# Two pairs of heads behind one exponential: four PSUM banks in one tile

## The chip, the cores and the metric

The program runs on one core of one Trainium2 chip. The metric is the device time of one execution in microseconds; the kernel before takes 1420.18 us (median of 3 runs, 1420.05 to 1421.76). A profile of one further execution is read beside it. Engines are named as in the profile: PE is the matrix engine (PEld its weight loads), ACT the engine that evaluates the exponentials, DVE the vector engine, POOL the engine that does the causal masks here, SP the queue that issues most of the DMAs.

## The reference

Two attentions over 2048 tokens with 32 heads of 18 dimensions are computed and their outputs laid side by side. A has one shared key and value head; B is causal inside four segments of 512 tokens and adds a linear memory of the segments before.

```python
# A
scores = jnp.einsum("bhqd,bkd->bhqk", q, k) * (Dh ** -0.5)
p = _softmax(scores, axis=-1)
o = jnp.einsum("bhqk,bkd->bhqd", p, v)
# B, for each segment s
logits = jnp.einsum("bhqd,bhkd->bhqk", qs, ks) * scale + mask
p = _softmax(logits, axis=-1)
a_dot = jnp.einsum("bhqk,bhkd->bhqd", p, vs)
o = g * a_mem + (1.0 - g) * a_dot
```

## The kernel before

The first 290 us or so are the projections of A and B. What the change touches is the attention stage behind them, one straight line of instructions whose order on PE, ACT and DVE is written out by hand (`tc.manual_schedule`), engine by engine. A planner places semaphores and hands out buffers: an instruction that writes a tile for the first time waits until one of the tile's buffers has been read by its last reader.

**Blocks.** There are 32 A blocks (4 chunks of 512 queries, 8 groups of 4 heads) and 32 B blocks (4 segments, 8 groups), set one behind the other in the list `blocks`. In a block the work is cut into *items*: one key tile `kt` of 128 keys and one *pair* of heads, `pr` 0 or 1. An A block has 16 x 2 = 32 items, in the order (kt 0, pr 0), (kt 0, pr 1), (kt 1, pr 0) and so on, a B block 3 x 2 = 6.

**Turns.** Items are taken three at a time (`turns`, made by `split`, lines 1080 to 1096). An A block has ten turns of three and, last, one of two: turns 0 to 10 in this text. A B block has two turns of three, 0 and 1. There are 416 turns. In turn k the loop at line 1111 issues, in this order: the scores of the turn's items (PE), the exponentials (ACT), one step of an output projection of finished work (tile F; its eight matmuls are line 770), one step of an exponential that DVE computes by a polynomial (`slow`), and the products of turn k-2 (PE, line 967).

**Scores.** `scores()` writes the two heads of a pair into a PSUM tile `E` of two banks, 128 keys by 2 x 512 queries: two matmuls side by side in the array, each preceded by its weight load (line 919 for A, 928 for B). The pool `psE` holds three such tiles; tiles O (products) and F take the other two of the eight banks. The exponential (line 937) reads `E` and writes an SBUF tile `P`, of which there are `PBUFS` = 9. Of a turn's three items the middle one (`i == 1`, `copied`) is first copied by DVE into an SBUF tile `W` (line 934), which frees its banks, and its exponential reads `W`. ACT takes a turn's exponentials in the order 0, 2, 1 (line 1114). Item (kt 0, pr 1) of each A block, the middle one of turn 0, has no ACT exponential; DVE computes it in nine operations spread over the following turns into tile `PD`.

**Products.** `products(b, m, hf)` takes step m of a block and one half `hf` of the queries: four matmul calls, two heads of pair 0 and two of pair 1 (eight matmul instructions in the trace, here called a *group*), so a turn's products are three groups, 24 instructions. In A the key tile of step m is `turn_of[j // 2][m]`: for pair 0 it is m; for pair 1 the list starts at 1 (1, 2, ..., 12, 0, 13, 14, 15), since the DVE item comes late. Steps are cut into threes as the items are, except that the short one lies at place 8 (`prods`, cut two turns earlier). The last group that reads a `P` tile is what gives that buffer back.

**The end.** After the last turn the last two rows of A are projected with the tiles `E`, O and F as accumulators (line 1164), and the results leave through `P`, `W` and `osb`.

Of the kernel before, what the change touches and what calls it, by code (L numbers as in the profile page):

```python
# [7 lines left out]
F32 = mybir.dt.float32  # L8
F32R = mybir.dt.float32r
# [21 lines left out]
PBUFS = 9  # L31
# [40 lines left out]
def attention_pair_kernel(ctx, tc, a_xT, a_w, a_wo, b_xT, b_w, b_wo, b_beta, ident_d, hmask_d, bmask_d, cmask_d, sel_d, zmask_d, selx_d, sely_d, out):  # L72
# [601 lines left out]
    psE = ctx.enter_context(tc.tile_pool(name="psE", bufs=3, space=PSUM))  # L674
# [231 lines left out]
    def scores(it, pr, copied):  # L906

        ab, c, hg, kt = it
        st = stacks[ab, c, hg // 2]
        h = 2 * (hg % 2) + pr  # L910
        e = psE.tile([128, 2, 512], F32, name="E")
        dve = ab == "A" and (kt, pr) in BY_DVE
        p = pp.tile([128, 2, 512], F32, name="PD" if dve else "P", bufs=1 if dve else PBUFS)
        state[it, pr] = p
        n = 512 if ab == "A" else 512 - 128 * kt if kt < 2 else 384
        if ab == "A":
            for j, r0 in enumerate(HALF):
                rows = slice(r0, r0 + KR)
                nc.tensor.matmul(e[:, j], kstA[rows, 128 * kt : 128 * kt + 128], st[rows, h, :], start=True, stop=True)  # L919
            if (kt, pr) in BY_DVE:  # L920
                exponentials(p, e)
                return lambda: None
        else:
            for k, c0 in BKEYS[kt]:
                ks = slice(128 * k, 128 * k + 128)
                for j, r0 in enumerate(HALF):
                    rows = slice(r0, r0 + KR)
                    nc.tensor.matmul(  # L928
                        e[:, j, c0 : c0 + 512 - 128 * k], st[rows, 4 + h, ks], st[rows, h, 128 * k :], start=True, stop=True
                    )  # L930
        src = e
        if copied:
            src = pp.tile([128, 2, 512], F32, name="W", bufs=2)
            nc.vector.tensor_copy(src[:, :, :n], e[:, :, :n])  # L934

        def exponential():
            nc.scalar.activation(p[:, :, :n], src[:, :, :n], AF.Exp, scale=SCALE)  # L937
            if ab == "B":

                m = len(BKEYS[kt])  # L940
                diag = p.rearrange("p a (b t) -> p a b t", t=256)[:, :, 0:m, 0:128]
                nc.gpsimd.affine_select(  # L942
                    diag, diag, pattern=[[0, 2], [0, m], [1, 128]], base=0, channel_multiplier=-1, compare_op=ALU.is_ge, fill=0.0
                )

        return exponential
# [140 lines left out]
    with tc.manual_schedule(engines={ENG.PE, ENG.Activation, ENG.DVE}):  # L1087
# [23 lines left out]
        for k in range(len(turns) + 2):  # L1111
            now[0] = k
            exps = [scores(its[n], pr, i == 1) for i, (n, pr) in enumerate(turns[k])] if k < len(turns) else []
            for i in (0, 2, 1) if len(exps) == 3 else range(len(exps)):
                exps[i]()
# [36 lines left out]

        def halve_heads(key, t):
            R = RT[t]
            x = halves_of[key, t] = pp.tile([128, 2, 512], F32R, name="P", bufs=PBUFS)
            halve(x[:R, 0], x[:R, 1], parts[key][:R, t])
# [27 lines left out]
        for n, key in enumerate(rows):  # L1184
            end = key == rows[-1]
            banks = [psE.tile([128, 2, 512], F32, name="E") for _ in range(3)]
            dst = [bk[:, hf, :288] for bk in banks for hf in range(2)]
# [8 lines left out]
            for i in range(4):  # L1196
                if end:
                    osb = pp.tile([128, 2, 512], F32, name="P", bufs=PBUFS)[:, :, :288]
                elif i < 2:
                    osb = pp.tile([128, 2, 512], F32, name="W", bufs=2)[:, :, :288]  # L1200
                else:
                    osb = pa.tile([128, D], F32, name="osb", bufs=2).rearrange("p (f n) -> p f n", f=2)
# [60 lines left out]
```

## Time and profile before

| | us |
|---|---|
| runs, median (lowest to highest) | 1420.18 (1420.05 to 1421.76) |
| the profiled execution, its own time | 1422.46 |
| span of its instructions | 1420.8 |
| DVE busy | 1034.9 |
| POOL busy | 248.5 |
| first to last score matmul of the attention stage | 292.8 to 1376.1 |

The profile is of one execution. A row of a group gives line, engine, operation, the tiles (written <- read), shapes and count, then the busy time, the mean duration of one in ns, and the engine's idle time just before them with what ended it. A row of the timeline gives start, length, engine, line and tiles, the number of instructions merged (x2), and in brackets the idle time before them. A timeline asked for a very short stretch shows the instructions that cross it, so single instructions can be told apart. Matmuls are pipelined and their ends are modelled, so a busy PE is not PE at its peak.

### The profile page before, as it was taken

The page shows a single profiled execution, that of the slowest core. Times are in us where ns is not written, and L with a number is a line of the kernel's source. Part 1 is how long each engine was busy: PE and PEld are TensorE (multiplying, and loading weights), DVE is VectorE, ACT ScalarE, POOL GpSimd, SP SyncE. Part 2 cuts the span into 40 slices and gives each one's busy share as a digit, 9 for nine tenths or more (in the row PEclk, how much of TensorE's full clock was granted, in tenths as well). Part 3 has the DMA queues.
Part 4 walks back from the last instruction along what each step waited for, and adds up shares of the span by engine and source line. Part 5 has one row for each costly group of instructions (what it writes and reads, how often), then busy time and mean ns, then how long its engine had stood idle before and what let it go on. Part 6 is the DMA issues. An engine that isn't in the chain of part 4 may idle for free.

```text
span 1420.8 us, 40029 instructions
## 1 busy us (share of the span) xinstructions
PE 1404.1 (99%) x17132; PEld 844.8 (59%) x17132; DVE 1034.9 (73%) x1220; ACT 1205.0 (85%) x1448; POOL 248.5 (17%) x326
## 2 busy tenths in 40 slices
PE   9999999999999999999999999999999999999998
PEld 6788888745555555555555555555555555555558
DVE  6656456467787778877777888777778877887773
ACT  4543434479999999999999999999999999999991
POOL 2431000003313214221110160131011400100002
PEclk9999999999999999999999999999999999999999
DMA  9866546467565535332312542232104121110013
GB/s 271 268 207 187 166 144 219 168 175 223 154 212 160 168 117 162 90 113 77 111 58 70 165 131 91 67 107 75 51 34 135 64 75 47 59 44 18 9 60 111
DMA packets 90720, 172.63 MB, mean 122 GB/s; under 512 B 14576, under 2 KB 22889, under 8 KB 90110
## 3 DMA queue, kind: packets, MB, share of 16 engines
q1 hardware_dynamic: 83978, 159.75, 35.9%
q0 software_dynamic: 1664, 4.78, 1.3%
q10 hardware_dynamic: 4896, 5.51, 1.1%
q8 instruction: 135, 2.21, 0.7%
q14 instruction: 47, 0.39, 0.1%
HBM read 99.32 MB, written 70.67 MB: 120 GB/s over the span
## 4 chain that ended last, share of the span: by engine, by line
PE 67%; ACT 9%; issue 2%; DVE 1%; DMA 0%; POOL 0%; ACTq 0%; DVEq 0%
PE O L967 30%; PE E L919 19%; PE F L770 11%; ACT P L937 9%; PE E L928 3%; PE E L1164 2%; PE F L826 1%; DVE W L934 0%; DMA oA<-oe 0%; PE F L1164 0%; PE O L1164 0%; DMA sm<-oA 0%; POOL P L942 0%; DVE osb L794 0%; DVE o L831 0%
## 5 line engine op out<-in xcount | busy, mean ns | idle before, releaser
L937 ACT ACTIVATE P<-E 128x1024 f32<-128x1024 f32 (+1 forms) x800 | 781.7, 1062 | 11.7 <-PE E L919 11.6
L934 DVE COPY W<-E 128x1024 f32<-128x1024 f32 (+1 forms) x384 | 461.0, 1200 | 176.3 <-PE E L919 120.1
L967 PE MATMUL O<-P,VA 128*32 128x256 f32 x7936 | 508.3, 379 | 0.0
L937 ACT ACTIVATE P<-W 128x1024 f32<-128x1024 f32 (+1 forms) x384 | 427.9, 1114 | 3.9 <-DVE W L934 3.7
L967 PEld LDWEIGHTS O<-P,VA 128*32 128x32 f32 x7936 | 262.6, 110 | 146.5 <-issue 5.7
L919 PE MATMUL E<-stA,kstA 56*128 56x512 f32 x1920 | 329.0, 439 | 2.3 <-DVE W L934 1.3
L919 PEld LDWEIGHTS E<-stA,kstA 56*128 56x128 f32 x1920 | 154.9, 184 | 178.1 <-ACT P L937 112.4
L942 POOL TENSOR_SCALAR_AFFINE_SELECT P<-P 128x256 f32<-128x256 f32 (+1 forms) x192 | 94.6, 493 | 474.0 <-ACT P L937 441.5
L758 POOL TENSOR_TENSOR o<-o,rb 126x512 f32<-126x512 f32 (+1 forms) x55 | 81.9, 1504 | 410.2 <-DMA o<-oA 263.8
L770 PE MATMUL F<-woB,o 126*32 126x192 f32 (+1 forms) x1920 | 127.4, 338 | 0.3 <-DVE osb L794 0.3
L899 DVE SCALAR_TENSOR_TENSOR q<-q,PD 128x1024 f32<-128x1024 f32 x96 | 120.3, 1253 | 0.0
L967 PE MATMUL O<-P,vseg 128*32 128x256 f32 (+2 forms) x1536 | 81.8, 344 | 0.4 <-issue 0.3
L770 PEld LDWEIGHTS F<-woB,o 126*32 126x32 f32 (+1 forms) x1920 | 38.2, 108 | 70.7 <-issue 62.7
L976 DVE COPY oe<-O 128x512 f32<-128x512 f32 x64 | 44.2, 691 | 40.7 <-PE O L967 40.0
L249 PE MATMUL pj<-xh,wBl 128*126 128x512 f32 x180 | 72.4, 403 | 0.0
L249 PE MATMUL pj<-xh,wBh 128*126 128x512 f32 x180 | 71.8, 400 | 0.0
L118 ACT CAST qp<-pj 126x512 fp32r<-126x512 f32 (+1 forms) x54 | 30.9, 584 | 44.7 <-DVE kmB L447 32.9
L770 PE MATMUL F<-woA,o 126*32 126x192 f32 (+1 forms) x960 | 63.9, 338 | 0.0
L967 PEld LDWEIGHTS O<-P,vseg 128*32 128x32 f32 x1536 | 49.0, 109 | 24.9 <-issue 2.0
L928 PE MATMUL E<-stB 56*128 56x256 f32 (+3 forms) x512 | 61.2, 347 | 1.3 <-ACT P L937 0.9
L119 DVE TENSOR_TENSOR qp<-pj,qp 126x512 fp32r<-126x512 f32 (+1 forms) x54 | 36.6, 684 | 35.4 <-ACT qp L118 35.2
L249 PE MATMUL pj<-xl,wBh 128*126 128x512 f32 x144 | 57.3, 399 | 0.0
(193 smaller groups left out, 1388.6 us busy)
## 6 DMA issues: line engine op xcount, KB each, us to landing
stB<-kB SPq DMA_DIRECT2D x96, 144.0 KB
stB<-qB SPq DMA_DIRECT2D x32, 288.0 KB
stA<-qA SPq DMA_DIRECT2D x30, 288.0 KB
oA<-oe SPq DMA_DIRECT2D x32, 256.0 KB
oB<-oe SPq DMA_DIRECT2D x32, 256.0 KB
qA<-qp SPq DMA_DIRECT2D x16, 504.0 KB
kB<-qp SPq DMA_DIRECT2D x16, 504.0 KB
qB<-qp SPq DMA_DIRECT2D x16, 504.0 KB
```

The source lines that it names most:

```text
L119: hold(nc.vector.tensor_tensor(qp[:R, 1, :n], src, qp[:R, 0, :n].bitcast(F32), op=ALU.subtract))
L249: nc.tensor.matmul(dst, w[:, c0 : c0 + M], x, start=i == 0, stop=i == len(ops) - 1)
L758: return lambda: tc.keep_in_program_order(nc.gpsimd.tensor_tensor(dst, a, b, op=op))
L770: nc.tensor.matmul(dst[32 * j : 32 * j + 32], parts[ab, c][: RT[t], t, r0 : r0 + 32], wo[ab][: RT[t], t, c0 : c0 + n], start=start, stop=stop,
L899: steps.append(lambda a=a: v.scalar_tensor_tensor(q, q, a, p, op0=ALU.add, op1=ALU.mult))
L919: nc.tensor.matmul(e[:, j], kstA[rows, 128 * kt : 128 * kt + 128], st[rows, h, :], start=True, stop=True)
L928: nc.tensor.matmul(e[:, j, c0 : c0 + 512 - 128 * k], st[rows, 4 + h, ks], st[rows, h, 128 * k :], start=True, stop=True)
L934: nc.vector.tensor_copy(src[:, :, :n], e[:, :, :n])
L937: nc.scalar.activation(p[:, :, :n], src[:, :, :n], AF.Exp, scale=SCALE)
L942: nc.gpsimd.affine_select(diag, diag, pattern=[[0, 2], [0, m], [1, 128]], base=0, channel_multiplier=-1, compare_op=ALU.is_ge, fill=0.0)
L967: nc.tensor.matmul(o[32 * j : 32 * j + 32, q0 : q0 + n], v, p[:, j % 2, p0 : p0 + n], start=m == hf == 0, stop=last and hf == 1,)
L976: nc.vector.tensor_copy(osb, o)
```

## The change

The three two-bank tiles become one tile `E4` of four banks and one tile `E2` of two, each with a single buffer. A turn's scores go, first, for one item into `E2` (the middle one in an A turn of three, the last one in a B turn; none in a turn of two), then for the two others into the halves of `E4`. One exponential of 4 x 512 columns reads `E4` and writes an SBUF tile `P4` of twice the size. The single item keeps its way through `W` by DVE and its own exponential, now into `P2`, or DVE's polynomial. `P4` and `P2` have three buffers each, the space that nine `P` took. A turn of two has no copy any more. B's masks follow the joint exponential. At the end the accumulators are `E4` and `E2` in place of three `E`, and the last outputs leave through `W` and `osb` alone.

```diff
@@ -28,7 +28,7 @@
 BOUND_UP = 1.0 + 2.0 ** -6
 
 BOUND_OK = 30.0 / SCALE / BOUND_UP
-PBUFS = 9
+PBUFS = 3
 KP = 54
 KR = 56
 VW = DH + 1
@@ -671,7 +671,7 @@
 
     pp = ctx.enter_context(tc.tile_pool(name="pp", bufs=1))
     pa = ctx.enter_context(tc.tile_pool(name="pa", bufs=1))
-    psE = ctx.enter_context(tc.tile_pool(name="psE", bufs=3, space=PSUM))
+    psE = ctx.enter_context(tc.tile_pool(name="psE", bufs=1, space=PSUM))
     psO = ctx.enter_context(tc.tile_pool(name="psO", bufs=1, space=PSUM))
 
     def load_stackA(c, q4):
@@ -903,47 +903,76 @@
         ]
         slow.extend((now[0] + 2 + i, p, step) for i, step in enumerate(steps))
 
-    def scores(it, pr, copied):
+    def width(it):
+
+        return 512 if it[0] == "A" else 512 - 128 * it[3] if it[3] < 2 else 384
+
+    def score(it, pr, e):
 
         ab, c, hg, kt = it
         st = stacks[ab, c, hg // 2]
         h = 2 * (hg % 2) + pr
-        e = psE.tile([128, 2, 512], F32, name="E")
-        dve = ab == "A" and (kt, pr) in BY_DVE
-        p = pp.tile([128, 2, 512], F32, name="PD" if dve else "P", bufs=1 if dve else PBUFS)
-        state[it, pr] = p
-        n = 512 if ab == "A" else 512 - 128 * kt if kt < 2 else 384
         if ab == "A":
             for j, r0 in enumerate(HALF):
                 rows = slice(r0, r0 + KR)
                 nc.tensor.matmul(e[:, j], kstA[rows, 128 * kt : 128 * kt + 128], st[rows, h, :], start=True, stop=True)
-            if (kt, pr) in BY_DVE:
-                exponentials(p, e)
-                return lambda: None
-        else:
-            for k, c0 in BKEYS[kt]:
-                ks = slice(128 * k, 128 * k + 128)
-                for j, r0 in enumerate(HALF):
-                    rows = slice(r0, r0 + KR)
-                    nc.tensor.matmul(
-                        e[:, j, c0 : c0 + 512 - 128 * k], st[rows, 4 + h, ks], st[rows, h, 128 * k :], start=True, stop=True
-                    )
-        src = e
-        if copied:
-            src = pp.tile([128, 2, 512], F32, name="W", bufs=2)
-            nc.vector.tensor_copy(src[:, :, :n], e[:, :, :n])
+            return
+        for k, c0 in BKEYS[kt]:
+            ks = slice(128 * k, 128 * k + 128)
+            for j, r0 in enumerate(HALF):
+                rows = slice(r0, r0 + KR)
+                nc.tensor.matmul(
+                    e[:, j, c0 : c0 + 512 - 128 * k], st[rows, 4 + h, ks], st[rows, h, 128 * k :], start=True, stop=True
+                )
+
+    def mask(it, p):
+
+        if it[0] == "B":
+            m = len(BKEYS[it[3]])
+            diag = p.rearrange("p a (b t) -> p a b t", t=256)[:, :, 0:m, 0:128]
+            nc.gpsimd.affine_select(
+                diag, diag, pattern=[[0, 2], [0, m], [1, 128]], base=0, channel_multiplier=-1, compare_op=ALU.is_ge, fill=0.0
+            )
+
+    def scores(items):
+
+
+        two, one = ((0, 2), 1) if items[0][0][0] == "A" and len(items) == 3 else ((0, 1), 2)
+        if one < len(items):
+
+            it1, pr1 = items[one]
+            e1 = psE.tile([128, 2, 512], F32, name="E2")
+            score(it1, pr1, e1)
+        e = psE.tile([128, 4, 512], F32, name="E4")
+        p = pp.tile([128, 4, 512], F32, name="P4", bufs=PBUFS)
+        pair = [(items[i], p[:, 2 * x : 2 * x + 2]) for x, i in enumerate(two)]
+        for x, ((it, pr), px) in enumerate(pair):
+            state[it, pr] = px
+            score(it, pr, e[:, 2 * x : 2 * x + 2])
+        n = width(items[0][0])
+        assert width(items[two[1]][0]) == n
 
         def exponential():
-            nc.scalar.activation(p[:, :, :n], src[:, :, :n], AF.Exp, scale=SCALE)
-            if ab == "B":
-
-                m = len(BKEYS[kt])
-                diag = p.rearrange("p a (b t) -> p a b t", t=256)[:, :, 0:m, 0:128]
-                nc.gpsimd.affine_select(
-                    diag, diag, pattern=[[0, 2], [0, m], [1, 128]], base=0, channel_multiplier=-1, compare_op=ALU.is_ge, fill=0.0
-                )
-
-        return exponential
+            nc.scalar.activation(p[:, :, :n], e[:, :, :n], AF.Exp, scale=SCALE)
+            for (it, pr), px in pair:
+                mask(it, px)
+
+        if one >= len(items):
+            return [exponential]
+        m = width(it1)
+        if it1[0] == "A" and (it1[3], pr1) in BY_DVE:
+            p1 = state[it1, pr1] = pp.tile([128, 2, 512], F32, name="PD", bufs=1)
+            exponentials(p1, e1)
+            return [exponential]
+        p1 = state[it1, pr1] = pp.tile([128, 2, 512], F32, name="P2", bufs=PBUFS)
+        src = pp.tile([128, 2, 512], F32, name="W", bufs=2)
+        nc.vector.tensor_copy(src[:, :, :m], e1[:, :, :m])
+
+        def exponential1():
+            nc.scalar.activation(p1[:, :, :m], src[:, :, :m], AF.Exp, scale=SCALE)
+            mask(it1, p1)
+
+        return [exponential, exponential1]
 
     acc = {}
 
@@ -1110,9 +1139,8 @@
         wparts = []
         for k in range(len(turns) + 2):
             now[0] = k
-            exps = [scores(its[n], pr, i == 1) for i, (n, pr) in enumerate(turns[k])] if k < len(turns) else []
-            for i in (0, 2, 1) if len(exps) == 3 else range(len(exps)):
-                exps[i]()
+            for step in scores([(its[n], pr) for n, pr in turns[k]]) if k < len(turns) else []:
+                step()
             if memory is None:
                 run_fill()
             elif k >= ASK and all(its[n][0] == "A" for n, pr in turns[k]) and next(memory, None) is None:
@@ -1150,9 +1178,18 @@
         assert len(rows) == 2 and all(ab == "A" for ab, c in rows)
         halves_of = {}
 
+        spare = []
+
         def halve_heads(key, t):
             R = RT[t]
-            x = halves_of[key, t] = pp.tile([128, 2, 512], F32R, name="P", bufs=PBUFS)
+            if not spare:
+
+                if len(halves_of) == 6:
+                    spare.extend(pp.tile([128, 2, 512], F32R, name="P2", bufs=PBUFS) for _ in range(3))
+                else:
+                    x = pp.tile([128, 4, 512], F32R, name="P4", bufs=PBUFS)
+                    spare.extend((x[:, 0:2], x[:, 2:4]))
+            x = halves_of[key, t] = spare.pop(0)
             halve(x[:R, 0], x[:R, 1], parts[key][:R, t])
 
         def multiply(key, t, dst):
@@ -1183,8 +1220,8 @@
             halve_heads(rows[1], t)
         for n, key in enumerate(rows):
             end = key == rows[-1]
-            banks = [psE.tile([128, 2, 512], F32, name="E") for _ in range(3)]
-            dst = [bk[:, hf, :288] for bk in banks for hf in range(2)]
+            banks = [psE.tile([128, n, 512], F32, name=f"E{n}") for n in (4, 2)]
+            dst = [bk[:, i, :288] for bk in banks for i in range(bk.shape[1])]
             dst += [psO.tile([128, C], F32, name=nm)[:, :288] for nm in ("O", "F")]
             for t in range(5):
                 while end and weighed[key] <= t:
@@ -1194,9 +1231,7 @@
                     halve_heads(key, t)
                 multiply(key, t, dst)
             for i in range(4):
-                if end:
-                    osb = pp.tile([128, 2, 512], F32, name="P", bufs=PBUFS)[:, :, :288]
-                elif i < 2:
+                if i < 2:
                     osb = pp.tile([128, 2, 512], F32, name="W", bufs=2)[:, :, :288]
                 else:
                     osb = pa.tile([128, D], F32, name="osb", bufs=2).rearrange("p (f n) -> p f n", f=2)
```

## The prediction

> **What bounds the kernel now.** I read the page first, for the engines' shares.
>
> ```profile
> span 1420.8 us, 40029 instructions
> ...
> PE 1404.1 (99%) x17132; PEld 844.8 (59%) x17132; DVE 1034.9 (73%) x1220; ACT 1205.0 (85%) x1448; POOL 248.5 (17%) x326
> ...
> ACT  4543434479999999999999999999999999999991
> ...
> L937 ACT ACTIVATE P<-E 128x1024 f32<-128x1024 f32 (+1 forms) x800 | 781.7, 1062 | 11.7 <-PE E L919 11.6
> ...
> L937 ACT ACTIVATE P<-W 128x1024 f32<-128x1024 f32 (+1 forms) x384 | 427.9, 1114 | 3.9 <-DVE W L934 3.7
> L967 PEld LDWEIGHTS O<-P,VA 128*32 128x32 f32 x7936 | 262.6, 110 | 146.5 <-issue 5.7
> ```
>
> From slice 9 on ACT is full, and its 1184 exponentials (800 + 384) waited only 15.6 us in all. PE shows 99% too. To see which of them sets the pace I then took the timeline of single turns. First ACT, one exponential per row, and the same with 768 columns:
>
> ```profile
> 697.23 1.11 ACT L937 ACTIVATE P<-E 128x1024 f32<-128x1024 f32 x1
> ...
> 698.13 1.15 ACT L937 ACTIVATE P<-W 128x1024 f32<-128x1024 f32 x1
> ...
> 699.08 1.12 ACT L937 ACTIVATE P<-E 128x1024 f32<-128x1024 f32 x1
> ...
> 699.98 1.13 ACT L937 ACTIVATE P<-E 128x1024 f32<-128x1024 f32 x1
> ...
> 711.74 0.98 ACT L937 ACTIVATE P<-E 128x768 f32<-128x768 f32 x1
> ...
> 712.43 0.99 ACT L937 ACTIVATE P<-E 128x768 f32<-128x768 f32 x1
> ```
>
> Read the starts, not the lengths: one exponential lasts 1.11 but the next starts 0.90 after it (0.95 after one that reads `W`). A turn of three costs ACT 0.90 + 0.90 + 0.95 = 2.75 us. 256 columns fewer start 0.69 apart, so a column costs (0.90 - 0.69) / 256 = 0.82 ns, 1024 of them 0.84, and 0.06 of each start-to-start step is fixed.
>
> Then PE, in a turn in which it waits for nobody, and in one in which it does:
>
> ```profile
> 554.61 0.96 PE L919 MATMUL E<-stA,kstA 56*128 56x512 f32 x6
> ...
> 555.50 0.53 PE L770 MATMUL F<-woB,o 126*32 126x192 f32 x8
> ...
> 555.85 1.48 PE L967 MATMUL O<-P,VA 128*32 128x256 f32 x24
> ...
> 557.26 0.50 PE L919 MATMUL E<-stA,kstA 56*128 56x512 f32 x2
> ...
> 694.47 1.10 ACT L937 ACTIVATE P<-E 128x1024 f32<-128x1024 f32 x1
> ...
> 695.62 0.19 PEld L919 LDWEIGHTS E<-stA,kstA 56*128 56x128 f32 x2 [0.29 <-ACT P L937]
> ...
> 696.05 0.53 PE L770 MATMUL F<-woB,o 126*32 126x192 f32 x8
> ```
>
> Alone, PE needs 557.26 - 554.61 = 2.65 us for a turn of three, hardly less than ACT's 2.75. In the second turn the third pair of score matmuls stood until the exponential that reads its banks was over (694.47 + 1.10 = 695.57; weights at 695.62, 0.05 later). So the bound is both engines, closely balanced, with ACT ahead by a little. A whole A block shows it: these two rows stand at the same place of consecutive blocks.
>
> ```profile
> 1234.86 1.02 ACT L937 ACTIVATE P<-E 128x1024 f32<-128x1024 f32 x1 [0.24 <-PE E L919]
> ...
> 1263.86 1.02 ACT L937 ACTIVATE P<-E 128x1024 f32<-128x1024 f32 x1 [0.24 <-PE E L919]
> ...
> 292.80:1376.10 1083.30, 1077.24 (x15244) 574.75 (x15244) 849.11 (x841) 1068.64 (x1181) 196.47 (x261) 1.00 0.33 100
> ```
>
> A block is 29.00 us, 11 turns; 32 of them are 928 of the stage's 1083.3 us (last row, a windows view: its length, then busy PE, PEld, DVE, ACT, POOL, clock 1.00), which leaves 155.3 / 64 = 2.43 us for a B turn. These two rows also give what an exponential lasts when ACT was idle before it: 1.02.
>
> **The change part by part.** *Fewer exponentials.* Two of 1024 cost ACT 1.80, one of 2048 costs 1.80 - 0.06 = 1.74: at most 0.06 x 416 turns = 25 us, if ACT still sets the pace. The Trainium skill says the same and a warning with it ("Perfetto Trace Analysis", Optimizing Scalar/DVE Operations): about 51 ns of fixed overhead for ScalarE on PSUM, larger operations help a saturated engine, but where the engine is not saturated and makes bubbles on others, smaller pieces may finish the work sooner. By its figure the gain would be at most 0.051 x 416 = 21 us, by the trace's 25; what the warning is worth here, the next part measures.
>
> *One buffer of four banks.* The joint exponential of turn k must be over before PE may write `E4` of turn k+1, and PE must have written all of it before the next may start. That loop has four terms:
>
> ```profile
> 695.03 0.72 PE L919 MATMUL E<-stA,kstA 56*128 56x512 f32 x4
> ...
> 1205.33 0.50 PE L919 MATMUL E<-stA,kstA 56*128 56x512 f32 x2
> ...
> 1205.87 1.02 ACT L937 ACTIVATE P<-E 128x1024 f32<-128x1024 f32 x1 [0.24 <-PE E L919]
> ```
>
> From ACT's end to the weights 0.05 (above); two pairs of score matmuls from the first weight load 0.72 (first row); from their end to ACT 0.04 (1205.33 + 0.50 to 1205.87); and the exponential. It is not in the trace: 1.02 + 0.84 = 1.86 after an idle ACT, 1.11 + 0.84 = 1.95 in a dense stream. I take 1.90, between them, as ACT will stand idle in part of the turns; the loop is 2.71 (2.67 to 2.76). ACT's own work in a turn of three, 1.74 + 0.95 = 2.69, just covers it, and PE's 2.65 fits in, so in nine of eleven turns this costs nothing against 2.75. But turn 0 (the third exponential is DVE's) and turn 10 (two items) took less and now pay the whole loop: 11 x 2.71 = 29.8 against 29.0 a block, +0.8, times 32 = **+26 us**. In a B block turn 0 pays 2.71, turn 1 about 2.3 (an estimate: its exponential has 512 columns fewer, 0.42, and its `E4` is written by six matmuls in place of four): 2.5 against 2.43, **+5 us** in 64 turns. "Independent matmul groups should rotate through different PSUM banks" is the skill's rule (same page, Matmuls); by it alone the kernel would come out at about 1451, the first rival.
>
> *`P4` with three buffers.* This is the part that costs. A tile `P4` holds items 0 and 2 of a turn and comes back only when both are used up. Follow one: turn 0 of an A block holds (kt 0, pr 0) and (kt 1, pr 0). The latter belongs to product step 1, halves 0 and 1, the block's groups number 2 and 3 (from 0). Group 3 is the first of the three that are issued in turn 3. So `P4` of turn 0 is free after the first group of turn 3, `P4` of turn 1 (its (kt 2, pr 1) serves the same step 1) at the same moment, and that of turn 2 (up to kt 4) only in turn 5. Turn 3 wants a buffer, none is free, and its exponential has to wait for the first group of the products *of its own turn*, which PE issues behind these very scores and the step of F. In turn 4 one is free already. Going on through the list, turns 3, 5, 7 and 9 of each A block wait so (4 x 32 = 128). At block borders, where the short product turn shifts things, turn 1 of the 18 A blocks that follow an A block and turn 1 of 13 B blocks that follow an A block wait likewise, and turn 0 of the same 31 blocks waits for the second group. In all 128 + 31 + 31 = 190 turns of 416. Before, the same groups gave back single tiles, and only the second exponential of a turn needed them:
>
> ```profile
> 699.16 0.62 PE L967 MATMUL O<-P,VA 128*32 128x256 f32 x8
> ```
>
> This is the first group of the turn whose exponentials start at 699.08 and 699.98: it ends at 699.78, 0.2 before the second one starts, and well after the first, which needed nothing of it. Joined, both must start after it.
>
> The price of one such wait, from the first weight load of `E4`: one pair that had to wait takes 696.05 - 695.62 = 0.43 to the start of F, a second pair 0.22 more (0.72 - 0.50), together 0.65; F to O 0.35 (555.50 to 555.85); the group 0.62; to ACT 0.04: 1.66. In the plain loop the exponential starts 0.72 + 0.04 = 0.76 after that weight load. So a gated turn costs 0.90 more; a turn without a step of F, of which there are about one in ten (2880 matmuls of line 770 in the rows below make 360 steps of eight; 24 more belong to the memory; 416 turns), 0.55. Mean 0.87. A second group adds a third of the products, (557.26 - 555.85) / 3 = 0.47. Nothing gives it back: the next `E4` is written only after this late exponential ends, so the loop starts again from there.
>
> ```profile
> L770 PE MATMUL F<-woB,o x1920: 323/326/351, 444.2 to 1382.6; 126*32 126x192 f32 x192
> ...
> L770 PE MATMUL F<-woA,o x960: 326/338/351, 761.2 to 1230.3; 126*32 126x192 f32 x168, 72*32 72x192 f32 x24
> ```
>
> 190 x 0.87 + 31 x 0.47 = 165 + 15 = **+180 us**.
>
> *Costed at nothing.* The scores for `W` move to the front of PE's order, and the exponential of `W` comes 1.74 after the joint one starts; the copy is over by then, and the one polynomial step queued behind it on DVE still fits a turn of 2.7:
>
> ```profile
> L934 DVE COPY W<-E 128x1024 f32<-128x1024 f32 (+1 forms) x384 | 461.0, 1200 | 176.3 <-PE E L919 120.1
> ...
> L899 DVE SCALAR_TENSOR_TENSOR q<-q,PD 128x1024 f32<-128x1024 f32 x96 | 120.3, 1253 | 0.0
> ...
> L976 DVE COPY oe<-O 128x512 f32<-128x512 f32 x64 | 44.2, 691 | 40.7 <-PE O L967 40.0
> ```
>
> Counted from the first weight load of `E4`, the scores for `W` end at about 0.2 (0.50 long, begun some 0.3 before), the copy at 1.4, and its exponential begins at 0.76 + 1.74 = 2.5: a microsecond to spare, and 1.20 + 1.25 is under 2.7. If that cover went, ACT would wait in its order and the loop would grow by the same time. The products that read `P2` of the turn before are the second group, 0.65 + 0.35 + 0.47 = 1.5 us after the weights of `E4`, and that exponential (1.15 long, begun 0.16 before the joint one's end) is over 1.0 after its end. The masks on POOL come later by up to one exponential and have a turn's time. No DMA moves but the last outputs.
>
> **The sum.** The profiled execution took 1422.46 us (1.7 around its span of 1420.8). 1422.5 + 26 + 5 + 180 = 1633.5; that execution stands 2.3 over the median of the runs, so the forecast is 1631, rounded to **1630 us**. Terms off at the same time (exponential 1.86 or 1.95 in 416 turns: -17 to +21; a gate of 0.8 to 1.0 in 190: -13 to +25) give 1605 to 1680 for this case alone.
>
> **The rivals.** *The buffers do not gate*: the planner finds a free buffer, and only the loop of `E4` counts. 1420 + 26 + 5 = 1451. For it: the trace before shows no exponential that waited for products. Against: there the single tiles were free 0.2 earlier than needed. If half of the gates go (ACT late for other reasons, so that the group is over), 1451 + 89 = 1540.
>
> *Faster after all*: `E4`'s banks come back to PE while the exponential is still reading, bank by bank. Then the loop is hidden, the gates find ACT already behind, and each A block falls to what PE needs alone, 10 x 2.65 and 1.99 for the turn of two (its four score matmuls to the next turn's first):
>
> ```profile
> 706.13 0.73 PE L919 MATMUL E<-stA,kstA 56*128 56x512 f32 x4
> ...
> 708.12 1.12 PE L928 MATMUL E<-stB 56*128 56x512 f32 x6
> ```
>
> That makes 28.5, 0.5 less than now, 16 us in 32 blocks: 1404. It decides if PE's weight loads for `E4` start before the exponential ends. Against it stands the row at 695.62: the weight load itself waited until 0.05 after the exponential's end.
>
> *More goes wrong than the gate*: PE idles between, and DVE's steps (copy 1.20, polynomial 1.25, at a block's end another 0.69) fall so that the copy into `W` comes late in each gated turn. Half a microsecond more in 190 turns: 1630 + 95 = 1725.
>
> **How the numbers follow.** Gate and loop as worked out 0.65, 1605 to 1680; a third to two thirds of the gates 0.10, 1505 to 1575; no gates 0.10, 1451; more 0.10, 1690 to 1725; faster 0.05, 1404. The range 1500 to 1710 holds the first, the partly gated case and about half of the heavier one: 0.65 + 0.10 + 0.05, eight in ten. A measurement of this kernel tells 0.2%, 2.8 us, from no change: faster 0.05, within 0.01, slower 0.94.
>
> **What would show it.** In the changed profile: joint exponentials of 128x2048 with about 1.9 us each; ACT no longer full, its idle time before them ended by the products (line of O) in about 190 cases of some 0.8 us, and by the scores in most others by little; weight loads of `E4` released by ACT with PE idle before; A blocks of about 29.8 + 4 x 0.87 = 33.3 us, in which turns alternate between 2.7 and 3.6. Wrong would be: equal turns near 2.7 (no gate), weight loads of `E4` inside a running joint exponential, or idle time of ACT that ends with DVE's copy.

## The result, and the profile after

| | before | after |
|---|---|---|
| runs beside each other, median (lowest to highest), us | 1420.58 (1420.05 to 1421.76), 4 runs | 1654.31 (1653.90 to 1654.97), 4 runs |
| the profiled execution, its own time, us | 1422.46 | 1654.64 |
| its span, us | 1420.8 | 1652.9 |

After divided by before is 1.1644, with a 95% interval of 1.1624 to 1.1665: 233.7 us slower. The forecast was 1630 us, in a range of 1500 to 1710.

The page of the changed kernel, in the rows that answer to those of before (line 937 has become 956 for the joint exponential and 972 for the one that reads `W`; 919 has become 918, 967 is now 996):

```profile
span 1652.9 us, 39464 instructions
...
PE 1458.5 (88%) x17132; PEld 845.1 (51%) x17132; DVE 987.0 (60%) x1188; ACT 1210.5 (73%) x1032; POOL 242.4 (15%) x326
...
ACT  4443343788888887788888877888887778888882
...
L956 ACT ACTIVATE P<-E 128x2048 f32<-128x2048 f32 (+1 forms) x416 | 767.8, 1846 | 240.1 <-PE O L996 218.0
...
L918 PE MATMUL E<-stA,kstA 56*128 56x512 f32 x1920 | 369.8, 459 | 143.9 <-ACT P L956 142.2
L972 ACT ACTIVATE P<-W 128x1024 f32<-128x1024 f32 (+1 forms) x352 | 355.8, 1011 | 0.0
```

ACT is no longer full from slice 9 on. It is busy as long as before (1210.5 us, 1205.0 before) but stands idle 240.1 us ahead of the joint exponentials, and 218.0 of that ended with the products, line 996. The score matmuls now wait 142.2 us for the joint exponential. Each engine waits for the other in turn, and none of them is the bound. The exponentials that read `W` did not wait at all (0.0).

The view of everything at line 956 tells how often:

```profile
L956 ACTq EVENT_SEMAPHORE  x417: 17/17/38, 293.1 to 1608.2; - x139
L956 ACT ACTIVATE P<-E x416: 1450/1878/1887, 294.3 to 1608.3; 128x2048 f32<-128x2048 f32 x130, 128x1536 f32<-128x1536 f32 x9
its engine sat idle before it (us, times) until:
  PE O L996: 218.0, 190
  PE E L918: 17.9, 29
  PE E L924: 2.3, 14
```

The second row is count, shortest, median and longest duration in ns: a joint exponential lasts 1.88 us. Exactly 190 of them waited for the products, and they are the turns on record: turns 3, 5, 7 and 9 of every A block, and turns 0 and 1 of the 18 A and 13 B blocks that follow an A block. The first row will matter below: nearly every joint exponential (414 of 416) has a semaphore instruction of its own in ACT's sequence.

Where the time went can be read in two neighbouring turns, on ACT and then on PE:

```profile
1101.49 1.88 ACT L956 ACTIVATE P<-E 128x2048 f32<-128x2048 f32 x1 [0.83 <-PE O L996]
1103.27 1.05 ACT L972 ACTIVATE P<-W 128x1024 f32<-128x1024 f32 x1
1104.26 1.88 ACT L956 ACTIVATE P<-E 128x2048 f32<-128x2048 f32 x1
1106.03 1.05 ACT L972 ACTIVATE P<-W 128x1024 f32<-128x1024 f32 x1
1107.91 1.88 ACT L956 ACTIVATE P<-E 128x2048 f32<-128x2048 f32 x1 [0.82 <-PE O L996]
```

```profile
1103.42 0.73 PE L918 MATMUL E<-stA,kstA 56*128 56x512 f32 x4 [0.74 <-ACT P L956]
...
1106.19 0.30 PEld L918 LDWEIGHTS E<-stA,kstA 56*128 56x128 f32 x4 [0.16 <-ACT P L956]
1106.19 0.73 PE L918 MATMUL E<-stA,kstA 56*128 56x512 f32 x4
1106.85 0.53 PE L770 MATMUL F<-woB,o 126*32 126x192 f32 x8
1107.20 0.62 PE L996 MATMUL O<-P,VA 128*32 128x256 f32 x8
```

From 1101.49 to 1104.26 a turn takes 2.77; from 1104.26 to 1107.91 it takes 3.65. In the longer one the joint exponential ends at 1106.14, the weights of the next `E4` are loaded 0.05 later, and the two pairs of scores are written by 1106.92. `E4` is full then, and ACT is through with the exponential of `W` at 1107.08, but the next exponential still waits for a buffer `P4`. It comes with the first group of products, behind the step of F: 1107.20 + 0.62 = 1107.82. The exponential starts 0.09 after that. In the shorter turn it started 0.11 after the scores (1103.42 + 0.73 = 1104.15, then 1104.26).

Nearly the whole loss, 231 of 234 us, lies in the attention stage: from the first score matmul to the last it takes 1314.0 us (1083.3 before).

```profile
294.30:1608.30 1314.00, 1131.14 (x15246) 574.62 (x15250) 802.43 (x810) 1076.14 (x768) 191.05 (x261) 1.00 0.27 83
```

For later use, the median length of each turn of a block, worked out from the timelines of three kernels, from a turn's first score matmul to the next turn's (a wait of ACT so shows one turn late; the third kernel is that of experiment 1):

```
turn            A0   A1   A2   A3   A4   A5   A6   A7   A8   A9   A10  | B0   B1
before          2.86 2.65 2.65 2.65 2.65 2.65 2.65 2.73 2.77 2.77 1.99 | 2.49 2.29
after           3.19 4.07 3.68 2.77 3.65 2.77 3.66 2.77 3.65 4.00 1.99 | 3.15 2.46
four P4         3.14 2.77 2.77 2.77 2.77 2.77 2.72 2.71 2.71 3.00 1.99 | 2.53 2.47
```

### The profile page after: what moved, and what is told of

The parts are those of the page before. It is cut to its first block, busy times and chain, and to the rows that moved or that the text cites. A ratio compares the mean times of both kernels' runs of the same rounds, so it can differ in the third digit from the quotient of the medians.

```text
span 1652.9 us, 39464 instructions
## 1 busy us (share of the span) xinstructions
PE 1458.5 (88%) x17132; PEld 845.1 (51%) x17132; DVE 987.0 (60%) x1188; ACT 1210.5 (73%) x1032; POOL 242.4 (15%) x326
## 3 DMA queue, kind: packets, MB, share of 16 engines
q0 software_dynamic: 1664, 4.78, 1.1%
## 4 chain that ended last, share of the span: by engine, by line
PE 49%; ACT 30%; issue 2%; DVE 0%; ACTq 0%; DVEq 0%
ACT P L956 28%; PE O L996 18%; PE E L918 17%; PE F L770 9%; PE E L924 3%; ACT P L972 2%; PE E L1201 1%; PE F L826 1%; ACTq L956 0%; PE F L1201 0%; PE O L1201 0%; DVE sm L726 0%; ACT W L1239 0%; DVE W L1239 0%; DVE W L969 0%
## 5 line engine op out<-in xcount | busy, mean ns | idle before, releaser
L956 ACT ACTIVATE P<-E 128x2048 f32<-128x2048 f32 (+1 forms) x416 | 767.8, 1846 | 240.1 <-PE O L996 218.0
L969 DVE COPY W<-E 128x1024 f32<-128x1024 f32 (+1 forms) x352 | 413.1, 1174 | 286.5 <-PE E L918 186.2
L918 PE MATMUL E<-stA,kstA 56*128 56x512 f32 x1920 | 369.8, 459 | 143.9 <-ACT P L956 142.2
L972 ACT ACTIVATE P<-W 128x1024 f32<-128x1024 f32 (+1 forms) x352 | 355.8, 1011 | 0.0
L933 POOL TENSOR_SCALAR_AFFINE_SELECT P<-P 128x256 f32<-128x256 f32 (+1 forms) x192 | 89.4, 493 | 624.1 <-ACT P L956 586.2
L924 PE MATMUL E<-stB 56*128 56x128 f32 (+3 forms) x512 | 71.2, 357 | 28.5 <-ACT P L956 27.8
L892 DVE TENSOR_SCALAR PD<-E 128x1024 f32<-128x1024 f32 x32 | 39.1, 1221 | 72.7 <-PE E L918 72.7
L924 PEld LDWEIGHTS E<-stB 56*128 56x128 f32 x512 | 40.2, 184 | 64.0 <-ACT P L956 40.3
```

What stands on the lines that cost most here:

```text
L924: nc.tensor.matmul(e[:, j, c0 : c0 + 512 - 128 * k], st[rows, 4 + h, ks], st[rows, h, 128 * k :], start=True, stop=True)
L933: nc.gpsimd.affine_select(diag, diag, pattern=[[0, 2], [0, m], [1, 128]], base=0, channel_multiplier=-1, compare_op=ALU.is_ge, fill=0.0)
L956: nc.scalar.activation(p[:, :, :n], e[:, :, :n], AF.Exp, scale=SCALE)
L969: nc.vector.tensor_copy(src[:, :, :m], e1[:, :, :m])
L972: nc.scalar.activation(p1[:, :, :m], src[:, :, :m], AF.Exp, scale=SCALE)
```

## The experiments

Two causes were on record, the wait for `P4` (180 us) and the loop of `E4` (31 us). The question was whether they are separate, and whether either can be had without the other. All kernels below compute the whole result. Runs of the kernel before on the same chips took 1421.87 us (experiments 1 to 4), 1422.72 (5 to 7) and 1422.42 (8 to 10). Each of these kernels was run once, the seventh four times; the kernel before ranged over 3.3 us beside them (1420.48 to 1423.79), so a difference of 2 or 3 us says nothing. Where a change needs room in SBUF, the tile `rb` (inverses of the softmax sums, 10 buffers of 512 columns, used off the path) gives up four buffers, exactly one `P4`.

**1. A fourth `P4`, and 2. only the smaller `rb`.** If the wait for `P4` costs what the forecast says, a fourth buffer takes it away and leaves the loop. The second kernel is the control.

```diff
-        p = pp.tile([128, 4, 512], F32, name="P4", bufs=PBUFS)
+        p = pp.tile([128, 4, 512], F32, name="P4", bufs=PBUFS + 1)
...
-        tiles = [pa.tile([128, C], F32, name="rb", bufs=10)]
+        tiles = [pa.tile([128, C], F32, name="rb", bufs=6)]
...
-            return loaded[0] + need <= 10
+            return loaded[0] + need <= 6
```

(The control has the lines of `rb` alone.)

> The changed kernel with four buffers for P4 in place of three (the space comes from the tile rb: six buffers in place of ten). Theory (the buffers gate): in the changed kernel a turn whose joint exponential waits for products takes 3.66 us and one that does not 2.77; 190 x 0.89 + 31 x 0.42 more where the second group is waited for = 182 us go, 1654 - 182 = 1472 us (1460 to 1485), and joint exponentials that wait for line O are gone. What is left over 1420.6, some 52 us, is the loop of E4. Rival (the single E4 alone, the products only happen to end the wait): 1654 us, unchanged.

> Control: the changed kernel with six buffers of the tile rb in place of ten, P4 as it was. Both theories: 1654 us, within 5; these buffers serve loads that are far ahead of their use.

Measured: 1470.58 us with four buffers, 1654.69 us for the control. First the page and the view of line 956 with four buffers, then the control's page:

```profile
L956 ACT ACTIVATE P<-E 128x2048 f32<-128x2048 f32 (+1 forms) x416 | 767.0, 1844 | 68.1 <-PE E L918 48.8
...
L956 ACTq EVENT_SEMAPHORE  x199: 17/17/38, 293.2 to 1405.5; - x199
```

```profile
L956 ACT ACTIVATE P<-E 128x2048 f32<-128x2048 f32 (+1 forms) x416 | 767.9, 1846 | 238.4 <-PE O L996 216.0
```

With four buffers no idle time of ACT ends with the products any more; the control keeps it all. Both are as expected. So of the 233.7 us the missing buffer is 1654.3 - 1470.6 = 184 (forecast 180) and the rest is 50 (forecast 31).

The timeline of ACT with four buffers shows what is left, across a block border:

```profile
1178.25 1.87 ACT L956 ACTIVATE P<-E 128x2048 f32<-128x2048 f32 x1
...
1180.96 1.88 ACT L956 ACTIVATE P<-E 128x2048 f32<-128x2048 f32 x1
1183.72 1.88 ACT L956 ACTIVATE P<-E 128x2048 f32<-128x2048 f32 x1 [0.89 <-PE E L918]
1186.49 1.88 ACT L956 ACTIVATE P<-E 128x2048 f32<-128x2048 f32 x1 [0.89 <-PE E L918]
...
1189.26 1.88 ACT L956 ACTIVATE P<-E 128x2048 f32<-128x2048 f32 x1
```

The last full turn of the block takes 2.71. Turn 10 (from 1180.96) and turn 0 (from 1183.72), which have a single exponential each, take 2.76 and 2.77: ACT stands for 0.89 in both, since the loop lasts as long as in a full turn. That is the cost the forecast gave to these two turns.

**3. Other pairs behind one exponential.** In an A turn that begins with pair 0 of a key tile past the first, items 0 and 1 (same key tile) share `E4`, and item 2 goes alone. By the order of the products only 63 joint exponentials are then left that need a `P4` still in use.

```diff
         two, one = ((0, 2), 1) if items[0][0][0] == "A" and len(items) == 3 else ((0, 1), 2)
+        if items[0] == (items[0][0], 0) and items[0][0][0] == "A" and items[0][0][3] > 0:
+            two, one = (0, 1), 2
```

> The changed kernel with the same number of buffers and operations; only which two items share a P4 differs: in turns 2, 4, 6, 8 and 10 of an A block items 0 and 1 (used up by the same product step) in place of 0 and 2. By the lists, 63 turns of 190 still wait (turn 3 of each block, turn 1 behind an A block), each for the first group. Theory: 96 waits of 0.89 and 31 of 1.31 go: 1654 - 85 - 41 = 1528 us (1510 to 1545). Rival (E4 alone): 1654 us.

Measured: 1532.54 us. The view of the joint exponentials' line (two lines on):

```profile
  PE O L998: 71.8, 63
```

63 waits, as counted from the lists, and the time is in the range expected. (One reason in the expectation is not exact: in turns 2 to 8 the products read items 0 and 1 one step apart, pair 1 first, not in the same step.) Without more memory, 127 waits fewer gave 1654.3 - 1532.5 = 122 us, 0.96 each. So the number of waits, not something else that the fourth buffer brings, sets the time. The remaining 62 us against the four buffers of experiment 1 would make 0.98 for each of 63, but a part of them goes with fewer semaphore instructions (below).

**4. Single tiles and single exponentials, `P4` as it is.** The three tiles `E` of two banks are back and each pair has its own exponential, but two of them write the halves of one `P4` with three buffers.

```diff
-        e = psE.tile([128, 4, 512], F32, name="E4")
...
+        es = []
...
-            score(it, pr, e[:, 2 * x : 2 * x + 2])
+            es.append(psE.tile([128, 2, 512], F32, name="E"))
+            score(it, pr, es[x])
...
-            nc.scalar.activation(p[:, :, :n], e[:, :, :n], AF.Exp, scale=SCALE)
+            for x, ((it, pr), px) in enumerate(pair):
+                nc.scalar.activation(px[:, :, :n], es[x][:, :, :n], AF.Exp, scale=SCALE)
```

> The changed kernel with three score tiles of two banks again and one exponential of 1024 columns for each, but the results of items 0 and 2 still share a P4 with three buffers. This leaves the shared buffer and takes away the loop. Theory: the waits for products stay (about 190), but PE runs ahead into free banks meanwhile, so that a waited turn and the next take about 6.1 in place of 5.5 us: 1420 + 190 x 0.5 = 1515 us (1470 to 1560). Rival (E4 alone): 1420 to 1430 us, as before the change.

Measured: 1605.39 us, above the range expected. Its page, and its table of waits (last two rows):

```profile
L958 ACT ACTIVATE P<-E 128x1024 f32<-128x1024 f32 (+1 forms) x832 | 794.7, 1014 | 183.2 <-PE O L998 174.4
...
PEld E L918 <- ACT P L958: 209.9, 478, 1.2
ACT P L958 <- PE O L998: 174.4, 190, 2.0
```

The same 190 waits, without any joint exponential, and 174.4 us in place of 218.0. The expectation had let PE run ahead while ACT stands; it can't, since the scores of the next pairs need the very banks that ACT has not read yet: the weight loads of line 918 wait 209.9 us for ACT here, and 80.7 in experiment 5, where the buffers are not short. So the shortage of result buffers needs no joint exponential to do its damage; how much of the time is its part, experiment 5 tells.

**5. The same with four `P4`.** What is then left against before is the order of the scores (the single item first on PE) and the missing copy in turn 10.

> The kernel with three score tiles and single exponentials again, and P4 with four buffers (rb six): neither the loop of E4 nor the wait for the shared buffer is left, only the new order of the scores. Theory: 1421 us (1415 to 1432), as before the change; the single tiles and the buffers together are the whole loss. Rival (something else in the change costs, the order with the copied item first on PE, or items 0 and 2 sharing a tile at all): well above 1432 us.

Measured: 1452.98 us, 32 more than expected, and 152 less than experiment 4; so much do the 190 waits cost there, 0.80 each where 0.5 had been expected. The timeline of ACT at a block border:

```profile
1201.67 1.94 ACT L958 ACTIVATE P<-E 128x1024 f32<-128x1024 f32 x2 [1.25 <-PE E L918]
```

ACT stands for 1.25 ahead of this block's first exponentials; in the kernel before the corresponding wait was 0.24 (the rows of 1234.86 and 1263.86 in the prediction). PE writes the pair that DVE will read first, and the pair that ACT waits for behind it.

**6. Turn 10 without the joint exponential.** Experiment 1, with the second item of the turn of two going through `E2`, `W` and its own exponential:

```diff
+        if len(items) == 2:
+            two, one = (0,), 1
...
+        c = 2 * len(two)
...
-            nc.scalar.activation(p[:, :, :n], e[:, :, :n], AF.Exp, scale=SCALE)
+            nc.scalar.activation(p[:, :c, :n], e[:, :c, :n], AF.Exp, scale=SCALE)
```

> The kernel with four P4 buffers (1470.6 us), but a turn of two items is not joined: item 0 alone in the first half of E4 with an exponential of 1024 columns, item 1 by E2 and the copy W, as before the change. Theory (what is left of the loss is the loop of E4 in turns that used to be shorter than it): a turn of two takes PE's 1.99 in place of 2.76 us, 0.77 x 32 = 25 us less, 1446 us (1440 to 1453). Rival (the loop costs a little in every turn alike): under 8 us less, 1463 to 1470 us.

Measured: 1443.38 us, as expected. So 27 of the 50 us of the loop hang on turn 10's joint exponential. That is near the 26 of the forecast, but those were for turns 10 and 0 together, and turn 0 keeps its joint exponential here. The 21 us that stay over the kernel before are about what turns 1 to 5 of the A blocks pay: 21 us more than before in all 32 blocks together, with four buffers and here alike.

**7. Two tiles of three banks.** A try at a better kernel: a turn's six banks as two tiles of three, two exponentials of 1536 columns, no copy into `W`, eight result tiles of three.

```diff
+        e = [psE.tile([128, 3, 512], F32, name="E3") for _ in range(2)]
+        p = [pp.tile([128, 3, 512], F32, name="P3", bufs=PBUFS) for _ in range(2)]
...
+                nc.scalar.activation(p[x][:, j0:j1, :n], e[x][:, j0:j1, :n], AF.Exp, scale=SCALE)
```

> Joint exponentials of three banks (1536 columns, one and a half pairs), two score tiles of three banks, two exponentials a turn, no copy by W, eight result tiles of three banks (rb six). Theory (a joint exponential pays where PE can fill another tile meanwhile and no buffer is late): ACT needs 2 x (1.26 + 0.06) = 2.64 us a turn, an A block 31 x 0.84 + 21 x 0.06 = 27.3 us, less than PE alone, 10 x 2.65 + 1.99 = 28.5; so PE sets 28.5 to 28.8 a block against 29.0: 1420 - 6 to 16, 1404 to 1414 us. Rival (larger exponentials always make PE wait longer for its banks): slower than before, 1430 us and more.

Measured: 1561.26 us (1559.89 to 1561.69), 1.0977 times the kernel before (95% interval 1.0958 to 1.0997). The expectation was wrong by 150 us. First ACT (two turns are merged in each row), then PE in the same stretch:

```profile
1198.84 5.52 ACT L969 ACTIVATE P<-E 128x1536 f32<-128x1536 f32 x4 [0.56 <-PE E L918]
1204.92 5.53 ACT L969 ACTIVATE P<-E 128x1536 f32<-128x1536 f32 x4 [0.56 <-PE E L918]
```

```profile
1207.76 0.72 PE L918 MATMUL E<-stA,kstA 56*128 56x512 f32 x3 [0.21 <-ACT P L969]
1208.41 0.53 PE L770 MATMUL F<-woA,o 126*32 126x192 f32 x8
1208.76 1.48 PE L994 MATMUL O<-P,VA 128*32 128x256 f32 x24
...
1210.17 1.05 PE L918 MATMUL E<-stA,kstA 56*128 56x512 f32 x6
```

Two turns take 6.08 us (1198.84 to 1204.92), where two full turns before took 2 x 2.65 to 2.77. In every second turn the second half of the scores waits for an exponential to end (0.21); F and the products stand behind it in PE's order, and ACT has run dry for 0.56 when the next scores come. The copy into `W`, which hands banks back to PE early, is missing here; that it is the missing copy that costs the time is argued, as no run puts it back.

**8. Experiment 5 with the old order.** The scores are issued in the order of the items again, and turn 10 has its copy:

```diff
-        if one < len(items):
-
-            it1, pr1 = items[one]
-            e1 = psE.tile([128, 2, 512], F32, name="E")
-            score(it1, pr1, e1)
+        if len(items) == 2:
+            two, one = (0,), 1
...
+            if one < len(items) and x == (one == 2):
+                it1, pr1 = items[one]
+                e1 = psE.tile([128, 2, 512], F32, name="E")
+                score(it1, pr1, e1)
```

> The kernel of 1453 us (three score tiles, single exponentials, P4 with four buffers), with two small parts of the change undone: A's scores in the order of the items again (before, the single item went first), and in a turn of two the second item goes through the copy W again. Theory (its 32 us over the kernel before are the block border: turns 10 and 0 of an A block take 1.98 + 3.54 = 5.5 us there, 1.99 + 2.86 = 4.85 before, as the scores that ACT waits for come one pair later and the last tile comes back late): 0.67 x 32 = 21 us less, 1432 us (1422 to 1436), the rest in B. Rival (items 0 and 2 sharing one result tile costs even with four buffers): still 1450 us.

Measured: 1424.56 us. ACT at a block border, then its page:

```profile
1177.52 1.94 ACT L959 ACTIVATE P<-E 128x1024 f32<-128x1024 f32 x2 [0.30 <-PE E L918]
```

```profile
L959 ACT ACTIVATE P<-E 128x1024 f32<-128x1024 f32 (+1 forms) x800 | 789.0, 1071 | 14.6 <-PE E L918 14.5
```

The wait at the border is back at 0.30, and the time is within 2 us of the kernel before, as near as single runs tell. A shared result tile costs nothing that shows once there are four of them and the banks come back pair by pair. Order and copy together were 1453.0 - 1424.6 = 28, where 21 had been expected; which of the two it is was not tried apart.

**9 and 10. The kernel before with eight and with six `P`.** Three `P4` and three `P2` hold as many items as nine `P`. How many does the old form need?

```diff
-PBUFS = 9
+PBUFS = 8
```

> The kernel before with PBUFS 8 in place of 9, nothing else. By the lists the third item's exponential of every second A turn then has to wait for the first group of its own turn. In the timeline of before that group ends at 699.78 and the exponential starts at 699.98, so the wait is hidden. Theory: 1421 us, 1419 to 1428. Rival (result buffers don't matter at all): the same.

> The kernel before with PBUFS 6: in every second A turn the first exponential waits for the first group of its own turn (699.82 against 699.08: 0.74 us late) and the third for the last group, in the other turns for the second. Theory: at least 160 x 0.74 = 118 us more, 1540 us (1520 to 1620), with exponentials that wait for line O, though every score tile is single and of two banks. Rival (the loss is in the banks of PSUM, not in result buffers): 1421 to 1430 us.

Measured: 1421.28 us with eight, 1672.41 us with six. The pages, of eight and then of six:

```profile
L937 ACT ACTIVATE P<-E 128x1024 f32<-128x1024 f32 (+1 forms) x800 | 784.7, 1061 | 11.7 <-PE E L919 10.5
```

```profile
L937 ACT ACTIVATE P<-E 128x1024 f32<-128x1024 f32 (+1 forms) x800 | 770.8, 997 | 190.1 <-PE O L967 181.1
L937 ACT ACTIVATE P<-W 128x1024 f32<-128x1024 f32 (+1 forms) x384 | 398.8, 1039 | 40.4 <-PE O L967 40.4
```

Eight single buffers are enough, so one of the nine was spare. Six cost 250 us, with 181.1 + 40.4 = 221.5 us of ACT's idle time ending with the products; that is more than the 1540 (to 1620) expected. The changed kernel, with room for nine items, loses 184 us to its result buffers (152 with single score tiles) and so comes out nearer to six single buffers than to nine: a `P4` whose one half is done with is not free.

## Why the prediction was right

**The wait for `P4`: right, in mechanism, count and size.** 190 waits were read off the order of the products, and 190 were found, in the same turns. The extra time of a waiting turn was put at 0.90 with a step of F; the timeline has 3.65 against 2.77, 0.88. The sum was 180, and the fourth buffer gives 184 (about 13 of them are not the waits', see the next paragraph). Experiment 3 takes away two thirds of the waits without any memory, and the time follows; experiment 10 makes such waits in the kernel before.

**The loop of `E4`: right in mechanism, mis-sized.** Three of its four terms hold: 0.05 from ACT's end to the weights (1106.14 to 1106.19), 0.73 for two pairs of scores (0.72 forecast), 1.88 for the exponential (1.90). The fourth, "from their end to ACT 0.04", was taken from an exponential of the kernel before that waited for one thing only. A joint exponential waits for its scores and for its buffer. In the changed kernel it starts 0.11 after the scores (above), and the view of line 956 has 417 semaphore instructions, one for nearly every exponential. With four buffers there are 199, and there both kinds of turn can be seen side by side; this is PE, in a stretch that goes with the ACT rows of experiment 1:

```profile
1180.18 0.73 PE L918 MATMUL E<-stA,kstA 56*128 56x512 f32 x4 [0.22 <-ACT P L956]
...
1185.65 0.19 PEld L918 LDWEIGHTS E<-stA,kstA 56*128 56x128 f32 x2 [0.16 <-ACT P L956]
...
1185.99 0.40 PE L918 MATMUL E<-stA,kstA 56*128 56x512 f32 x2
```

Turn 10's scores end at 1180.91 and its exponential starts 0.05 later, at 1180.96. Turn 1's end at 1186.39 (the second pair, 1185.99 + 0.40) and its exponential starts 0.10 later, at 1186.49. In that whole trace the 195 joint exponentials with a semaphore instruction of their own (the very first left out) start 0.10 to 0.13 after the last of their scores, but for one at 0.39, and the 220 others 0.04 to 0.07. A full turn is 1.88 + 0.05 + 0.73 + 0.05 = 2.71, as forecast, in the one case and 2.77 in the other; both values stand in the table of turns (A7 and A8 against A1 to A5). For the changed kernel, where nearly every joint exponential is of the second kind, 416 x 0.06 = 25 us, and 1654 - 1630 = 24. That the two agree so closely is partly luck. The fourth buffer takes away 417 - 199 = 218 semaphore instructions together with the 190 waits, so by the same 0.06 about 13 of its 184 us are theirs and 171 are left for the waits (forecast 180); of the 50 us that stay 12 are theirs, and 38 are left for the loop (forecast 31). These two misses nearly cancel. The extra term can be seen in single turns too: a block of A behind another of A was forecast at 11 x 2.71 + 5 x 0.87 + (0.87 + 0.47) = 35.5; with 11 x 0.06 it is 36.2, and the table's row adds up to 36.2. That the difference goes with a second wait is shown; no run took the second wait away from a turn and left all else. (Of the forecast's own sums one is off: its terms added up make the narrow range 1601 to 1677, not 1605 to 1680.)

**Where the loop is paid: near in the sum, only in part right in the place.** The forecast had it in turns 0 and 10 and a little in B, and nothing in the nine full turns of A, as 2.71 is no more than ACT's 2.75. By the table four buffers cost an A block 30.1 - 29.0 = 1.1, times 32 is 35 (forecast 26), and a pair of B turns 5.00 - 4.78 = 0.22, times 32 is 7 (forecast 5); with all blocks added up in place of medians it is 34 and 11, and 3 more lie behind the last score matmul. But turns 9, 10 and 0 together are 8.13 against 7.62, 0.51 of the 1.1. Most of the rest is in turns 1 to 5: before, they ran at PE's 2.65 and not at ACT's 2.75, and now they take 2.77. The step that failed here is the price of nothing for full turns; the sum came near because the loop was taken for all eleven turns, 11 x 2.71, against a measured block.

**The joint exponential saves next to nothing: right in its effect.** Its gain was put at 25 us at most, and none of it in the sum beyond the loop. From its start to the next exponential's it takes 1.78 (1101.49 to 1103.27) where two took 0.90 + 0.90 = 1.80: 0.02 in a turn, not 0.06. The Trainium skill ("Perfetto Trace Analysis", Optimizing Scalar/DVE Operations) warns that where ScalarE is not saturated but makes bubbles on other engines, breaking up instructions may let work be completed sooner. Experiment 6 agrees: with turn 10's joint exponential split again (its second pair by `W`), 27 us are gone. The 0.88 lost in each of 190 turns is another matter, for experiment 4 has the same 190 waits with single exponentials.

**Costed at nothing: right,** but for the order of the scores. The copy into `W` kept no exponential waiting (0.0 above). That the single item now comes first on PE and that turn 10 has no copy was seen only through the loop; with single tiles, where there is no such loop, the two together cost 28 us (5 against 8). These costs need not add: in the changed kernel the border has to wait for the loop as well.

**The rivals.** "The buffers do not gate" is the kernel of experiment 1: 1470.6, where the rival had 1451; the loop's missing 19 is the difference. "Faster after all" needed weights of `E4` inside a running exponential; in all turns but one they start 0.05 after its end, and never earlier. "More goes wrong" needed late copies; there are none (0.0 above).

## What to carry to other kernels

Before operations are joined, write down for every tile they read and write who gives it back and when: a joined tile comes back with its last part and has to be free for its first, so room for nine results in three double and three single buffers lost 184 us here, while eight single buffers lost nothing and six lost 250. Count the waits from the order of the instructions (190 here) and price one along the chain that restarts behind it; both can be done before anything is run. What a joined operation saves is its fixed part alone, here 0.02 to 0.04 us of 1.80, and it is easily lost in a turn that used to be shorter.

## What the runs showed of the hardware

With four buffers a joint exponential that waited for two or more semaphores started 0.10 to 0.13 us after the last matmul of its scores (one of 195 at 0.39), one that waited for a single one 0.04 to 0.07 after it (the ends of matmuls are modelled), and the former has a semaphore instruction of its own in ACT's sequence (417 in the changed kernel, 199 with four buffers). The weights of the next `E4` were loaded 0.05 us after the joint exponential's end. A joint exponential of 2048 columns lasts 1.88 us, against 1.02 for 1024 columns after an idle ACT: 0.86 for the second half, and 1.76 to 1.78 from its start to that of the next.
